# First batch of a retention and gMLP kernel: spatial columns 1 and 3 as seven products over pairs of blocks

## The chip, the cores and the metric

The kernel runs on one core of a Trainium2 chip. The time is the device time of one execution in microseconds; three executions were timed. Five engines work side by side, each through its own queue in order: TensorE (PE in the profile; PEld is its loading of weights), VectorE (DVE), ScalarE (ACT), GpSimd (POOL) and SyncE (SP), which here only issues DMAs.

## The reference

Two layers, for 4 batches of 768 positions. The first is a retention layer with 8 heads of 64:

```python
state = gamma * state + k[t] v[t]^T
y[t]  = scale * q[t] state            # x = y, heads side by side: 768 x 512
```

The second is a gated MLP whose gate mixes positions:

```python
h = relu(x @ w_in);  u, v = halves of h           # 512 columns each
v_n = (v - mean) / sqrt(var + 1e-6)               # over the columns
v_s = w_spatial @ v_n + b_spatial                 # over the 768 positions
out = (u * v_s) @ w_out
```

## The kernel before, in words

**Precision.** Most large products are done three times on split numbers: an operand is cut into a high part (rounded to fp32r by a copy on ACT) and a low part (the rest, a subtraction called `residue`), and high x high, high x low and low x high are added in PSUM (`split3`, L445). A product on whole float32 operands needs no split but more time on PE for each instruction.

**Retention.** Positions come in groups of 128, six to a batch (g = 0 to 23). `ret_set(g)` (S in the order text, L342) makes the scores of group g+1 and the state updates of group g, the two interleaved on PE; the updates read the values of group g, which must have been scaled by the decay. It ends with the scaling of the values of group g+1 on POOL (`scale_values`, L289) and the mask on DVE. `ret_out(g)` (X, L438) makes the output of the group: small 64x64 matmuls on PE, eviction into xf on DVE, xh on ACT (`out_half`, L429) and xl on POOL. The xh and xl of three groups (384 positions, one half of a batch) share one tile; there are two buffers of each, so the third half takes the buffer of the first when everything that reads that one is done.

**MLP.** `mlp_u(b, j, half)` (u or U, L579) makes block j (128 columns) of u, transposed, for one half of the positions: 12 matmuls and a relu on ACT. `units` numbers the pairs: 0 to 3 are the blocks in half 0, 4 to 7 in half 1. `v_products` (V) makes v for one group of positions; relu, mean and variance, a power on POOL and the normalisation (N) follow. `mlp_out` (o, O, L641) adds the part of one unit to the output of its half, in three PSUM banks, and stores the half after its fourth unit.

**The spatial product.** v_s of a block of columns is a product over six blocks of positions, in two halves of the output. There are two ways in the code. `spatial_products` (P, L598) takes one unit: six whole float32 matmuls, or 18 split ones where the column block has been split before by `norm_split` (D, L502). `combine` and `product` (C, L514, and M, L540) take a pair of column blocks p and p+2 in both halves: Winograd's form of Strassen's scheme, seven products of half size instead of eight, each of nine split matmuls. Its left sides are pieces of v_n, some of them sums made in place on POOL, copied on ACT and subtracted on DVE; its right sides are the spatial weight's quarters and their sums and differences, made once by `split_spatial` (W0 to W6, L224): for each of three rows a copy on ACT and a residue on DVE, ahead of them a sum on DVE for W3 to W6. W3 to W6 overwrite the whole weight or read overwritten parts, so a `spatial_products` on whole numbers must come before them. Batches 1 to 3 use the seven products for both pairs (columns 0 and 2, then 1 and 3).

**Batch 0 before.** Its four units of half 0 go by whole numbers in START (P1, P0, P3, P2). In FIRST, `item` (I4 to I7, L674) does unit 4 whole and units 5 to 7 on columns split by D1 to D3. W0 to W6 are spread over all of FIRST.

**Order.** The order is written out by hand in the texts START, FIRST, REST and LAST: each word is an action, carried out in turn when the program is built. In START every instruction is tied to the one before it on its engine. From FIRST on, only matmuls, loads, the splits of the weights and the scaling of values are tied (`tc.keep_in_program_order`): a tied instruction is queued behind whatever the text put before it on that engine, tied or not. The rest is placed by a scheduler at build time. S, X, G and J of FIRST with number n mean group n; batch 0 is being finished there while groups 7 to 13 of batches 1 and 2 are loaded and the retention of batch 1 runs (S6 to S12, X6 to X11, V0 to V5).

**Weights.** The input and output weights come as 64-bit floats, in twelve parts ("doubles", L139): loaded to a raw tile (L), made into two float32 parts by operations on ACT and DVE (a, c), rounded to the high part on ACT (H), and the rest computed by two subtractions and additions (R n, on POOL, or R 20+n, on DVE). Parts 4 to 7 are the column blocks of u's weight, 8 to 11 the row blocks of the output's.

**Buffers.** PSUM: two banks for scores and states, three for u, v, spatial products and, from FIRST on, the retention outputs, three for the outputs. The tag u has six buffers, t three, v three (v before its normalisation and output tiles share it), ca four (pieces, and W6's differences). Values of groups 2, 5 and 8 lie in the tile "third", in the room that W4's parts take later.

Of the kernel before, what the change touches and what calls it, by code (L numbers as in the profile page):

```python
# [10 lines left out]
F32R = mybir.dt.float32r  # L11
# [12 lines left out]
START = (  # L24
# [10 lines left out]
)  # L35
FIRST = (
    "S6 W0 I4 W1 D1 X6 J9 S7 G9 D2 I5 X7 J10 G10 D3 W2 S8 W3 I6 X8 S9 V0 G11 W4 I7 X9 J11 S10 "
    "G12 O7 N0 X10 W5 V1 V2 V3 N1 N2 J12 G13 S11 X11 J13 G14 V4 N3 S12 N4 V5 W6 N5"
)
# [22 lines left out]
def tile_retention_gmlp(  # L62
# [15 lines left out]
    P = 128  # L78
# [41 lines left out]
    def keep(ins):  # L120

        if fixed:
            tc.keep_in_program_order(ins)
# [9 lines left out]
    def residue(eng, out, whole, high):  # L133
        return eng.tensor_tensor(out, whole, high.bitcast(F32), ALU.subtract)  # L134

    def pick(n):
# [4 lines left out]
        for w, src in ((winv_w, w_inv), (winu_w, w_inu), (wout_w, w_out))  # L141
        for k in range(KT)
    ]
# [22 lines left out]
    def pair_room(dtype, name):  # L166
        return mpool.tile([P, 2, HC, P], dtype, tag="ca", name=name, bufs=4)

    rooms = []
    for n in ROOMS:  # L170
        t = slot(n, F32, f"room{n}").rearrange("p s c -> p (s c)")
        rooms += [t[:, :DM], t[:, DM : 2 * DM]]
    halves = {}

    def split_top(i):
# [48 lines left out]
    def split_spatial(n):  # L224
# [20 lines left out]
        for s in range(HC):  # L245
            tc.keep_in_program_order(nc.scalar.copy(high[:, s], wholes[s]))
            tc.keep_in_program_order(residue(nc.vector, low[:, s], wholes[s], high[:, s]))

# [252 lines left out]

    def norm_split(j):  # L502

        whole = vn[0][:, :, j * P : j * P + P]
        high, low = (
            pair_room(F32R, f"vn{i}_{j}").rearrange("p n s d -> p (n s) d") for i in range(2)
        )
        keep(nc.scalar.copy(high, whole))
        keep(residue(nc.vector, low, whole, high))
        columns[j] = high, low  # L510

    pieces = {}
# [60 lines left out]

    columns = {}
    gate = {}
# [22 lines left out]
    def spatial_products(b, j, half):  # L598
        dcol = slice(j * P, j * P + P)
        pp = ps_m.tile([P, DM], F32, tag="m", name=f"sp{b}_{j}_{half}")  # L600
        if not (half and j in columns):
            for s in range(NC):
                l, r = vn[b][:, s, dcol], whole_sp[half, s // HC][:, s % HC]
                mm(pp[:, :HALF], l, r, start=(s == 0), stop=(s == NC - 1))
        else:
            vh, vl = columns[j]
            split3(
                [
                    (
                        (vh[:, s], vl[:, s]),  # L610
                        tuple(parts_sp[s // HC][i][:, s % HC] for i in range(2)),
                    )
                    for s in range(NC)
                ],
                pp[:, :HALF],
            )
        gate[b, half, j] = pp

    def gate_product(b, j, half):
        pp, u = gate[b, half, j], us.pop((b, half, j))  # L620
        t = mpool.tile([P, HALF], F32, tag="t", name=f"t{b}_{j}_{half}", bufs=3)
        cols = slice(half * HALF, half * HALF + HALF)
        keep(nc.vector.tensor_tensor(t, pp[:, :HALF], bsp_t[:, cols], ALU.add))
        keep(nc.vector.tensor_tensor(t, t, u, ALU.mult))
        gate[b, half, j] = t

# [44 lines left out]
    units = [(j, half) for half in range(2) for j in range(NJ)]  # L671
    NU = len(units)

    def item(b, i):  # L674
        mlp_u(b, *units[i])
        if i + 1 < NU:
            mlp_u(b, *units[i + 1])
        spatial_products(b, *units[i])
        gate_product(b, *units[i])
        part_gate(b, i)  # L680
        if i > 0:
            mlp_out(b, *units[i - 1])

    actions = {
# [7 lines left out]
        "N": lambda b, g, n: mlp_norm(b + 1, n),  # L692
        "I": lambda b, g, n: item(b, n),
        "O": lambda b, g, n: mlp_out(b, *units[n]),
        "D": lambda b, g, n: norm_split(n),
        "m": lambda b, g, n: load(mask_t, mask),
# [127 lines left out]
```

## Time and profile before

| | us |
|---|---|
| median of three runs | 374.7 (374.28 to 374.99) |
| the profiled execution | 374.61 |
| its span | 372.8 |
| mean granted clock of TensorE | 0.994 of full |

| stage on PE | start, us |
|---|---|
| first u block of batch 0 (u0) | 49.99 |
| first whole spatial block (P1) | 54.18 |
| end of u3; o2 follows | 78.00 |
| whole block of unit 4 | 85.52 |
| last v group of batch 1 (V5), end | 144.56 |
| first of the seven products of batch 1 | 159.19 |

The span runs from the first to the last instruction of the program; what lies around it in the profiled execution is 374.61 - 372.8 = 1.8 us. In the profile a line number is often that of a helper: L126 is every matmul, L134 every residue. A name such as `u<-xh,winu_w` says which tile is written and which are read, and a mean over a group can mix several uses. Names of PSUM tiles tell the stage: s and d are scores and state changes, x retention outputs, sp the products of `spatial_products`, y, z and w the banks of the seven products. A whole float32 matmul shows as two records, so 24 of them are x48.

### The profile page before, as it was taken

The page shows a single profiled execution, that of the slowest core. Times are in us where ns is not written, and L with a number is a line of the kernel's source. Part 1 is how long each engine was busy: PE and PEld are TensorE (multiplying, and loading weights), DVE is VectorE, ACT ScalarE, POOL GpSimd, SP SyncE. Part 2 cuts the span into 40 slices and gives each one's busy share as a digit, 9 for nine tenths or more (in the row PEclk, how much of TensorE's full clock was granted, in tenths as well). Part 3 has the DMA queues.
Part 4 walks back from the last instruction along what each step waited for, and adds up shares of the span by engine and source line. Part 5 has one row for each costly group of instructions (what it writes and reads, how often), then busy time and mean ns, then how long its engine had stood idle before and what let it go on. Part 6 is the DMA issues. An engine that isn't in the chain of part 4 may idle for free.

```text
span 372.8 us, 10291 instructions
## 1 busy us (share of the span) xinstructions
PE 362.0 (97%) x4418; PEld 317.3 (85%) x4418; DVE 236.4 (63%) x513; ACT 154.5 (41%) x308; POOL 134.4 (36%) x131
## 2 busy tenths in 40 slices
PE   6899999999999999999999999999999999999996
PEld 2778785787998878999998888999997888999985
DVE  3989989995887876677674543367674433165530
ACT  2486682264433535533124444432323445432232
POOL 1354650001343523526424451327424341325042
PEclk9899999999999999999999999999999999999999
DMA  7997783001431721113305332021504002000022
GB/s 265 411 371 278 243 310 156 0 2 54 147 114 58 273 89 69 54 61 109 122 2 199 114 114 86 8 106 47 185 0 143 2 2 86 0 0 2 0 86 85
DMA packets 13581, 41.49 MB, mean 111 GB/s; under 512 B 1888, under 2 KB 2144, under 8 KB 13536
## 3 DMA queue, kind: packets, MB, share of 16 engines
q1 hardware_dynamic: 13392, 40.71, 30.0%
q8 instruction: 35, 0.57, 0.6%
q10 hardware_dynamic: 144, 0.13, 0.1%
q14 instruction: 10, 0.08, 0.1%
HBM read 34.54 MB, written 6.29 MB: 110 GB/s over the span
## 4 chain that ended last, share of the span: by engine, by line
PE 94%; DMA 3%; issue 1%; DVE 1%; POOL 0%; SPq 0%; ACT 0%; POOLq 0%
PE u L126 18%; PE v L126 18%; PE o L126 18%; PE y L126 10%; PE sp L126 8%; PE x L126 7%; PE z L126 5%; PE s L126 3%; PE d L126 3%; PE w L126 3%; DMA qk<-in_groups_dram 2%; DMA vd_t<-in_vdecay_dram 2%; PE total L126 1%; PE o_last L126 0%; POOL vk L298 0%
## 5 line engine op out<-in xcount | busy, mean ns | idle before, releaser
L126 PE MATMUL u<-xh,winu_w 128*128 128x384 f32 x256 | 68.1, 338 | 0.0
L126 PE MATMUL v<-winv_w,xh 128*128 128x512 f32 x192 | 60.6, 397 | 0.2 <-issue 0.2
L126 PE MATMUL o<-wout_w,gh 128*128 128x512 f32 (+1 forms) x192 | 60.5, 396 | 0.0
L126 PEld LDWEIGHTS u<-xh,winu_w 128*128 128x128 f32 x256 | 46.5, 188 | 0.8
L126 PE MATMUL u<-xl,winu_w 128*128 128x384 f32 x128 | 42.9, 335 | 0.0
L134 POOL TENSOR_TENSOR xl<-xf,xh 128x512 fp32r<-128x512 f32 x21 | 29.0, 1380 | 37.6 <-ACT xh L436 37.6
L126 PEld LDWEIGHTS v<-winv_w,xh 128*128 128x128 f32 x192 | 35.2, 188 | 8.1 <-issue 0.4
L126 PE MATMUL y<-sp,a 128*128 128x384 f32 x216 | 41.6, 336 | 0.0
L126 PEld LDWEIGHTS o<-wout_w,gh 128*128 128x128 f32 x192 | 35.2, 188 | 7.3
L534 ACT CAST a<-vn 128x384 fp32r<-128x384 f32 x42 | 21.6, 513 | 46.0 <-PE y L126 16.9
L134 POOL TENSOR_TENSOR gl<-ur,gh 128x384 fp32r<-128x384 f32 x24 | 26.8, 1116 | 37.7 <-ACT gh L630 37.2
L134 DVE TENSOR_TENSOR a<-vn,a 128x384 fp32r<-128x384 f32 x42 | 24.4, 580 | 24.6 <-ACT a L534 24.2
L126 PEld LDWEIGHTS y<-sp,a 128*128 128x128 f32 x216 | 38.1, 188 | 0.2
L126 PE MATMUL v<-winv_w,xl 128*128 128x512 f32 x96 | 37.5, 390 | 0.0
L126 PE MATMUL o<-wout_w,gl 128*128 128x512 f32 (+1 forms) x96 | 37.3, 389 | 0.0
L477 DVE BATCH_NORM_STATS2 bst<-vr 128x6 f32<-128x512 f32 x24 | 16.6, 691 | 29.3 <-ACT vr L470 29.1
L419 DVE SCALAR_TENSOR_TENSOR xf<-x,qg_t,qd_t 128x128 f32<-128x128 f32 x96 | 27.1, 343 | 10.3 <-PE x L126 10.3
L484 POOL TENSOR_TENSOR rs<-rs,mhalf 128x1 f32<-128x1 f32 x24 | 13.7, 573 | 44.0 <-DVE rs L479 41.8
L126 PE MATMUL s<-qk 64*64 64x64 f32 x768 | 27.4, 221 | 0.7 <-DMA qk<-in_groups_dram 0.7
L126 PEld LDWEIGHTS s<-qk 64*64 64x64 f32 x768 | 25.1, 137 | 2.9 <-DMA qk<-in_groups_dram 1.4
L500 ACT ACTIVATE vn<-vr,nb,rs 128x512 f32<-128x512 f32 x24 | 19.4, 814 | 17.4 <-DVE nb L489 16.4
L595 ACT ACTIVATE ur<-u 128x384 f32<-128x384 f32 x32 | 15.7, 490 | 25.9 <-PE u L126 25.7
(103 smaller groups left out, 669.8 us busy)
## 6 DMA issues: line engine op xcount, KB each, us to landing
qk<-in_groups_dram SPq DMA_DIRECT2D x24, 512.0 KB, 5.3
vk<-in_groups_dram SPq DMA_DIRECT2D x21, 512.0 KB, 4.4
out_dram<-ot SPq DMA_DIRECT2D x23, 256.0 KB, 2.1
wst<-in_w_sp_dram SPq DMA_DIRECT2D x4, 576.0 KB, 8.1
raw<-in_w_inv_dram SPq DMA_DIRECT2D x4, 512.0 KB, 6.5
raw<-in_w_inu_dram SPq DMA_DIRECT2D x4, 512.0 KB, 7.5
raw<-in_w_out_dram SPq DMA_DIRECT2D x4, 512.0 KB, 5.1
third<-in_groups_dram SPq DMA_DIRECT2D x3, 512.0 KB, 6.0
```

Of the source, the lines that this page charges most:

```text
L126: ins = nc.tensor.matmul(out, lhs, rhs, start=start, stop=stop, skip_group_check=shared)
L134: return eng.tensor_tensor(out, whole, high.bitcast(F32), ALU.subtract)
L419: nc.vector.scalar_tensor_tensor(xf[:, hp], t[hp % 2][:, hp // 2].rearrange("p i c -> p (i c)"), qg_t[:, c, hp : hp + 1], qd_t[:, hp], ALU ...
L477: keep(nc.vector.bn_stats(st, norm[b, c][0]))
L484: keep(nc.gpsimd.tensor_tensor(rs, rs, mhalf, ALU.pow))
L500: keep(nc.scalar.activation(vn[b][:, c], v, AF.Identity, bias=nb, scale=rs))
L534: nc.scalar.copy(t[:, 0], whole)
L595: keep(nc.scalar.activation(u, pu[:, :HALF], AF.Relu))
```

## The change

In batch 0, column blocks 0 and 2 keep the whole float32 way, in both halves, all in START (P2, P0, P6, P4). Column blocks 1 and 3 are done by the seven products of `combine` and `product` with b = 0 and p = 1, in FIRST, after W0 to W5 (W6 lies among the products). Of the three residues of each W, those of rows 0 and 2 go to POOL (`POOLED`); row 1 stays on DVE. u blocks 0 and 2 of both halves are computed in START (u0, u2, u4, u6), blocks 1 and 3 in FIRST (U5, U1, U7, U3). To suit this, the parts of u's and the output's weights are taken in the order 0, 2, 1, 3. `norm_split` and `item` go away; `gate_product` writes into u's buffer instead of t's. The low part of the output weights' last part moves from DVE to POOL (R31 to R11), two of the four low parts of the gate in START move to FIRST on POOL, and some words in the early part of START change places.

```diff
--- before.py
+++ after.py
@@ -22,20 +22,21 @@
 
 
 START = (
-    "L0 G0 a0 c00 c01 H0 v c02 m q0 L2 j0 p0 t00 k00 y00 y01 t01 R20 G1 L1 p1 a2 G2 c20 E0 q1 "
-    "h0 k01 c21 j1 t10 y10 a1 H2 k10 G3 c10 y11 p22 t11 c22 q2 c11 k11 c12 L3 l0 H1 q3 t20 k20 "
-    "E1 G4 R1 V00 j2 h1 t21 l11 p23 k21 y20 y21 L5 R2 j3 q4 t30 E2 a3 h2 j4 c30 V10 p24 V01 V11 "
-    "V02 L4 l12 c31 V20 a5 k30 y30 c32 t31 H3 k31 c50 G5 y31 q5 E3 t40 a4 j5 R3 V21 V12 k40 c40 "
-    "L6 c51 y40 p25 y41 t41 h3 l3 V03 a6 k41 c41 E4 c42 c52 r0 s0 G6 h4 l4 H4 V22 L8 R4 V13 V23 "
-    "r2 K0 t50 k50 y50 q6 s2 w2 r1 y51 E5 w0 p26 h5 s1 L9 V30 l15 V40 n0 N0 K1 L7 H5 V31 K2 B "
-    "n2 c60 a8 V32 V50 V33 V51 w1 V41 V42 c61 r3 n1 s3 H6 R5 N1 V52 L10 V43 N2 w3 n3 r4 s4 V53 "
-    "w4 r5 N3 s5 w5 n4 n5 c62 c80 R26 N4 N5 a7 c70 u0 a9 G7 c90 u1 j6 c91 a10 P1 c100 g1 P0 c81 "
-    "c82 H8 R28 P3 f1 g0 K3 L11 c101 f0 H10 d10 c92 H9 P2 c102 o0 R29 R30 c71 d11 H7 u2 c72 R27 "
-    "a11 g2 f2 d12 c110 c111 o1 G8 u3 g3 H11 c112 f3 d13 o2 R31"
+    "L0 G0 a0 c00 c01 H0 v c02 m q0 L2 j0 p0 t00 k00 y00 y01 t01 R20 G1 L1 p1 a2 G2 c20 E0 q1 h0 "
+    "k01 j1 t10 c21 y10 H2 a1 k10 G3 c10 y11 p22 t11 c11 c22 q2 k11 c12 L3 l0 H1 q3 t20 k20 E1 G4 "
+    "R1 V00 j2 h1 t21 l11 p23 k21 y20 y21 L5 R2 j3 q4 t30 E2 a3 h2 j4 c30 V10 p24 V01 V11 V02 L4 "
+    "l12 c31 V20 a5 k30 y30 c32 t31 H3 k31 c50 G5 y31 q5 E3 t40 a4 j5 R3 V21 V12 k40 c40 L6 c51 y40 "
+    "p25 a6 y41 t41 h3 l3 V03 k41 c41 E4 c42 c52 r0 s0 G6 h4 l4 H4 V22 L8 R4 V13 V23 r2 K0 t50 k50 "
+    "y50 q6 s2 w2 r1 y51 E5 w0 p26 h5 s1 L9 V30 l15 V40 n0 N0 K1 L7 H5 V31 K2 B n2 c60 a8 V32 V50 "
+    "V33 V51 w1 V41 V42 r3 n1 c61 s3 H6 R5 N1 V52 L10 V43 N2 c80 w3 n3 r4 s4 V53 w4 r5 N3 s5 w5 n4 "
+    "n5 c62 R26 N4 N5 a7 c70 u0 a9 G7 K3 c90 u2 j6 a10 P2 c100 c91 g2 P0 c81 H8 P6 f2 c92 g0 c82 "
+    "L11 c101 f0 H10 R28 d10 H9 P4 c102 o0 R29 c71 R30 d12 H7 u4 c72 R27 a11 g4 c110 c111 o2 c112 "
+    "G8 u6 g6 H11 R11"
 )
 FIRST = (
-    "S6 W0 I4 W1 D1 X6 J9 S7 G9 D2 I5 X7 J10 G10 D3 W2 S8 W3 I6 X8 S9 V0 G11 W4 I7 X9 J11 S10 "
-    "G12 O7 N0 X10 W5 V1 V2 V3 N1 N2 J12 G13 S11 X11 J13 G14 V4 N3 S12 N4 V5 W6 N5"
+    "U5 S6 U1 W0 X6 U7 W1 S7 G9 U3 W2 J9 X7 G10 J10 S8 W3 V0 X8 C11 W4 G11 V1 S9 W5 C15 C16 V2 M11 "
+    "C13 W6 M15 C17 M16 C12 M13 C14 M17 M12 M14 F1 N0 O1 F3 N1 X9 J11 S10 G12 O3 N2 F4 F6 V3 O4 O6 "
+    "X10 J12 F5 G13 N3 S11 O5 X11 J13 F7 V4 O7 V5 S12 G14 N4 N5"
 )
 REST = (
     "U0 U2 C01 U4 C05 C06 U1 U3 C03 X0 J2 S1 U6 G3 M01 C07 M05 C02 M06 C04 M03 M07 M02 C11 M04 "
@@ -139,7 +140,7 @@
     doubles = [
         (w[:, k, 0], w[:, k, 1], src[:, k])
         for w, src in ((winv_w, w_inv), (winu_w, w_inu), (wout_w, w_out))
-        for k in range(KT)
+        for k in (range(KT) if w is winv_w else (0, 2, 1, 3))
     ]
     raws = {}
 
@@ -171,6 +172,7 @@
         t = slot(n, F32, f"room{n}").rearrange("p s c -> p (s c)")
         rooms += [t[:, :DM], t[:, DM : 2 * DM]]
     halves = {}
+    POOLED = {(n, s) for n in range(7) for s in (0, 2)}
 
     def split_top(i):
         parts = raws.pop(i).bitcast(I32).rearrange("p (n w) -> p n w", w=2)
@@ -244,7 +246,7 @@
         parts_sp[n] = high, low
         for s in range(HC):
             tc.keep_in_program_order(nc.scalar.copy(high[:, s], wholes[s]))
-            tc.keep_in_program_order(residue(nc.vector, low[:, s], wholes[s], high[:, s]))
+            tc.keep_in_program_order(residue(nc.gpsimd if (n, s) in POOLED else nc.vector, low[:, s], wholes[s], high[:, s]))
 
     queries = {}
     keys = {}
@@ -499,16 +501,6 @@
         v, nb, rs = norm.pop((b, c))
         keep(nc.scalar.activation(vn[b][:, c], v, AF.Identity, bias=nb, scale=rs))
 
-    def norm_split(j):
-
-        whole = vn[0][:, :, j * P : j * P + P]
-        high, low = (
-            pair_room(F32R, f"vn{i}_{j}").rearrange("p n s d -> p (n s) d") for i in range(2)
-        )
-        keep(nc.scalar.copy(high, whole))
-        keep(residue(nc.vector, low, whole, high))
-        columns[j] = high, low
-
     pieces = {}
 
     def combine(b, p, m):
@@ -571,7 +563,6 @@
         gate_high(b, j, half)
         gate_low(b, j, half, nc.gpsimd)
 
-    columns = {}
     gate = {}
     us = {}
     acc = {}
@@ -598,22 +589,9 @@
     def spatial_products(b, j, half):
         dcol = slice(j * P, j * P + P)
         pp = ps_m.tile([P, DM], F32, tag="m", name=f"sp{b}_{j}_{half}")
-        if not (half and j in columns):
-            for s in range(NC):
-                l, r = vn[b][:, s, dcol], whole_sp[half, s // HC][:, s % HC]
-                mm(pp[:, :HALF], l, r, start=(s == 0), stop=(s == NC - 1))
-        else:
-            vh, vl = columns[j]
-            split3(
-                [
-                    (
-                        (vh[:, s], vl[:, s]),
-                        tuple(parts_sp[s // HC][i][:, s % HC] for i in range(2)),
-                    )
-                    for s in range(NC)
-                ],
-                pp[:, :HALF],
-            )
+        for s in range(NC):
+            l, r = vn[b][:, s, dcol], whole_sp[half, s // HC][:, s % HC]
+            mm(pp[:, :HALF], l, r, start=(s == 0), stop=(s == NC - 1))
         gate[b, half, j] = pp
 
     def gate_product(b, j, half):
@@ -621,8 +599,8 @@
         t = mpool.tile([P, HALF], F32, tag="t", name=f"t{b}_{j}_{half}", bufs=3)
         cols = slice(half * HALF, half * HALF + HALF)
         keep(nc.vector.tensor_tensor(t, pp[:, :HALF], bsp_t[:, cols], ALU.add))
-        keep(nc.vector.tensor_tensor(t, t, u, ALU.mult))
-        gate[b, half, j] = t
+        keep(nc.vector.tensor_tensor(u, t, u, ALU.mult))
+        gate[b, half, j] = u
 
     def gate_high(b, j, half):
         t = gate[b, half, j]
@@ -669,18 +647,6 @@
                 (nc.scalar if n else nc.sync).dma_start(out[b, rows, c], ot[:, c])
 
     units = [(j, half) for half in range(2) for j in range(NJ)]
-    NU = len(units)
-
-    def item(b, i):
-        mlp_u(b, *units[i])
-        if i + 1 < NU:
-            mlp_u(b, *units[i + 1])
-        spatial_products(b, *units[i])
-        gate_product(b, *units[i])
-        part_gate(b, i)
-        if i > 0:
-            mlp_out(b, *units[i - 1])
-
     actions = {
         "S": lambda b, g, n: ret_set(g + n),
         "Z": lambda b, g, n: ret_set(g + n, update=False),
@@ -690,9 +656,7 @@
         "W": lambda b, g, n: split_spatial(n),
         "K": lambda b, g, n: load_spatial(n),
         "N": lambda b, g, n: mlp_norm(b + 1, n),
-        "I": lambda b, g, n: item(b, n),
         "O": lambda b, g, n: mlp_out(b, *units[n]),
-        "D": lambda b, g, n: norm_split(n),
         "m": lambda b, g, n: load(mask_t, mask),
         "v": lambda b, g, n: [load(vd_t, vdecay), load(qg_t, qgroup), load(qd_t, qdecay)],
         "B": lambda b, g, n: load(bsp_t, b_sp),
```

## The prediction

> **What bounds the kernel now.** I read the page from the top, then the busy time by stretch, then the chain that ended last.
>
> ```profile
> span 372.8 us, 10291 instructions
> PE 362.0 (97%) x4418; PEld 317.3 (85%) x4418; DVE 236.4 (63%) x513; ACT 154.5 (41%) x308; POOL 134.4 (36%) x131
> PE 94%; DMA 3%; issue 1%; DVE 1%; POOL 0%; SPq 0%; ACT 0%; POOLq 0%
> 0.00:40.00 40.00, 33.24 (x749) 26.19 (x752) 31.60 (x62) 22.95 (x62) 14.71 (x16) 0.96 0.85 314
> 40.00:78.00 38.00, 38.00 (x231) 29.32 (x224) 34.31 (x76) 18.71 (x38) 10.84 (x12) 1.00 0.47 168
> 78.00:104.00 26.00, 26.00 (x403) 22.21 (x403) 20.39 (x42) 12.82 (x26) 4.67 (x4) 1.00 0.25 86
> 104.00:145.00 41.00, 40.67 (x643) 34.55 (x642) 30.93 (x74) 18.21 (x33) 18.65 (x17) 1.00 0.36 129
> ```
>
> The last four rows give, after the window's length, busy us of PE, PEld, DVE, ACT, POOL. TensorE (PE) is the bound. It idles 6.8 us in the first 40 us and almost never afterwards: 0.33 us from 40 to 145 us, the stretch that holds the whole first batch. So matmul time taken out of that stretch is worth its full length, unless a new wait of PE appears. The other engines have room on average; POOL worked only 4.67 of the 26 us from 78 to 104, exactly where the change sends it new work. Full shares don't show whether its order holds, so that is looked at apart.
>
> **The matmul time that goes.** Rows of the chain: start, length, what.
>
> ```profile
> 54.18 15.48 PE sp L126 x48
> 85.52 3.87 PE sp L126 x12
> 95.60 3.12 PE sp L126 x18
> 105.22 3.12 PE sp L126 x18
> 115.53 3.15 PE sp L126 x18
> ...
> 183.13 1.59 PE y L126 x9
> 192.56 1.59 PE y L126 x9
> 194.15 2.09 PE o L126 x9
> ```
>
> A block of columns in one half of the positions, in whole float32, costs 15.48 / 4 = 3.87 us; a block from split parts costs 3.12 us. Before, batch 0 has five of the first and three of the second: 15.48 + 3.87 + 3.12 + 3.12 + 3.15 = 28.74 us. After, P2, P0, P6, P4 stay whole (4 x 3.87 = 15.48), and the four block-halves of columns 1 and 3 become seven products of nine matmuls. Batch 1 does just that for its second pair: from 183.13 to 194.15, 11.02 us. Sum 26.50 us: **2.24 us less**.
>
> **What the new order does to PE's joints.**
>
> ```profile
> 69.66 2.08 PE o L126 x9
> 71.74 2.09 PE u L126 x12
> 78.00 2.08 PE o L126 x9
> 91.48 0.86 PE x L126 x48
> 93.29 2.31 PE u L126 x12
> 100.79 1.09 PE x L126 x64
> 102.94 2.28 PE u L126 x12
> 126.28 8.42 PE v L126 x36
> 134.69 0.02 issue
> 137.57 2.95 PE v L126 x12
> 144.56 10.43 PE u L126 x60
> ```
>
> A u group behind large matmuls takes 2.09 us, behind the 64x64 ones 2.28 to 2.31: a joint costs 0.2 us. FIRST's text had 8 such joints and has 10 (S6, S7, S8, X8, S9, S10, S11, X11, S12, X6, each ahead of a large group): **+0.4 us**. An X and S pair takes 102.94 - 100.79 = 2.15 us, but from 134.69 to 137.57, 2.88 us pass for S11 and X11: X11 stands right behind S11 and waits for its states. The new text puts O5 (2.08 us) between them, which covers it: **-0.73 us**. So far 2.24 - 0.4 + 0.73 = 2.57 us gained, about 372.0 us.
>
> **What is added in front of it.** Groups first (busy us, mean ns of one, idle ahead), then three groups with the shortest, median and longest ns, and two single instructions of POOL's timeline.
>
> ```profile
> L134 DVE TENSOR_TENSOR sp<-wst,sp 128x384 fp32r<-128x384 f32 x18 | 10.6, 635 | 2.6 <-ACT sp L246 2.5
> L532 POOL TENSOR_TENSOR vn<-vn 128x384 f32<-128x384 f32 x18 | 19.5, 1084 | 15.2 <-DVE a L134 12.6 <-ACT vn L500 2.5
> L484 POOL TENSOR_TENSOR rs<-rs,mhalf 128x1 f32<-128x1 f32 x24 | 13.7, 573 | 44.0 <-DVE rs L479 41.8 <-ACT vn L500 1.7 <-DVE nb L489 0.5
> L419 DVE SCALAR_TENSOR_TENSOR xf<-x,qg_t,qd_t 128x128 f32<-128x128 f32 x96 | 27.1, 343 | 10.3 <-PE x L126 10.3
> L134 POOL TENSOR_TENSOR df<-df,winu_w 128x512 f32<-128x512 f32 x2 | 2.6, 1288 | 1.0 <-ACT winu_w L207 1.0
> L624 DVE TENSOR_TENSOR t<-t,ur 128x384 f32<-128x384 f32 x8 | 4.5, 557 | 0.4
> L134 POOL TENSOR_TENSOR gl<-ur,gh x24: 999/1015/1342, 167.9 to 365.4; 128x384 fp32r<-128x384 f32 x24
> L134 POOL TENSOR_TENSOR xl<-xf,xh x21: 1275/1293/2289, 14.6 to 304.4; 128x512 fp32r<-128x512 f32 x21
> L436 ACT CAST xh<-xf x24: 608/621/624, 13.2 to 303.7; 128x512 fp32r<-128x512 f32 x24
> 95.41 1.29 POOL L134 TENSOR_TENSOR xl<-xf,xh 128x512 fp32r<-128x512 f32 x1 [3.12 <-ACT xh L436]
> 96.66 1.04 POOL L298 TENSOR_TENSOR third<-third,vd_t 128x512 f32<-128x512 f32 x1
> ```
>
> Fourteen spatial residues go from DVE (635 ns) to POOL. POOL never did this one; a gl residue has its shape, so 1.02 us (999 to 1342 ns). DVE is relieved of 8.9 us, worth nothing by itself, since PE is the bound. All splits now stand ahead of the products.
>
> Now the queue. A residue of W, and the scaling of the next group's values, are tied behind whatever the text put before them on POOL. The last two rows show it: scaling of group 8 (the tile third) starts the moment xl of group 6 is done. The new text reads X6, W1, S7, so POOL's order is xl of group 6, **two residues of W1**, scaling of group 8. And xl needs xh of group 6, which takes the buffer of batch 0's first half; u blocks 1 and 3 of that half still read it. Before, all four such u ran in START; now U1 and **U3** are in FIRST, and U3 stands behind X6, U7 and S7. Who waits at the end: S8, whose updates read group 8's scaled values, and with S8 all of PE, because its order is fixed.
>
> Times, with the rows above. The end of START holds the same groups as before (four u, four whole blocks, two o), so FIRST begins at 78.00. U5 2.09, S6 (2.15 - 1.09) 1.06, U1 2.28, X6 0.86, U7 2.28, S7 0.95 (93.29 - 91.48 - 0.86), U3 2.28: U3 ends at 89.80. X7 (1.09) ends at 90.89; there S8 wants to start. But after 89.80: handover 0.05 (assumed), xh 0.62, handover 0.05, xl 1.29, residues 2 x 1.02, scaling 1.04: 94.89. **PE waits 4.0 us.** With the shortest rows it is 3.9; with xl at 2289 ns and residues at 1342 ns 5.6. A cover that I can't exclude (xh free sooner) makes it 0. I take 4.0, since each link has a near row.
>
> Once S8 is through, the later parts are pressed but not clearly late. W5's residues come after W2, W3 and W4 on POOL; 94.9 + 8 residues (8.2) + xl 7 and 8 (2.6) + scaling of 9 and 10 (2.1) + two powers (2 x 0.57 = 1.1) ends near 109. M16, which reads W5, would start at 94.9 + S8 1.06, V0 to V2 with joints (3 x 2.95), X8 1.09, S9 1.06, M11 and M15 (3.1) = 110.1. That just fits, if the sums of C15 and C16 (L532's 1084 ns each, three of them) run while POOL waits for U3.
>
> **Edits taken at nothing.** Order 0, 2, 1, 3 of the weights: the same loads in the same places, each read no sooner than before. R11 on POOL instead of DVE: two operations at about 1.29 us (L134 df), begun at START's end by my estimate, so done near 81 us, ahead of the queue's wait. Gate product into u's buffer, dropped column splits (D), POOL gates of units 4 and 6: all under PE's 38 full microseconds and late use. K3 stands between G7 and L11 on SP in both texts, so its queue keeps its order. If DVE's cover (34.31 of 38 us) broke, u6 would lose up to a gate product, 2 x 0.56 = 1.1 us. The small swaps early in START lie where PE idles anyway; I take 0, between half a microsecond gained and lost.
>
> **Sum.** -2.24 + 0.4 - 0.73 + 4.0 = +1.4 us. The profiled execution took 374.61 us (span 372.8 and 1.8 around it), the median of the runs is 374.7; the forecast is **376.2 us**.
>
> **Rivals.**
>
> *The hold doesn't bind (faster).* One place decides: POOL's xl of group 6. If it starts before 90.89 - 1.04 - 2.04 - 1.29 = 86.5, scaling is done when PE comes to S8, and 372.1 us remains. X6 ends at 84.3 and DVE's four evictions (4 x 0.34) at 85.7, so without the hold by U3 this is what happens. For it: PE runs such products without a wait in batches 1 to 3, and had 0.33 us idle here. Against it: U3 after X6 is in the text, and in the later batches U3 stands ahead of X0. 371.5 to 373.3.
>
> *POOL is late a second time (slower still).*
>
> ```profile
> 104.54 1.34 DVE L233 TENSOR_TENSOR wst<-wst,wst 128x1152 f32<-128x1152 f32 x1
> 104.75 2.29 POOL L134 TENSOR_TENSOR xl<-xf,xh 128x512 fp32r<-128x512 f32 x1 [2.18 <-ACT xh L436]
> ```
>
> POOL's xl took 2.29 instead of 1.29 us while DVE formed a spatial sum: it lost about what was left of DVE's 1.34. If C15 and C16 don't go ahead, 3 x 1.08 = 3.3 us come behind W5, M16 waits about that long, and the clashes add to it: 376.2 + 3.3 = 379.5 us (377.8 to 381.5). [...]
>
> *A shorter wait that cancels the gain.* Should START end earlier, or one residue of W1 hide in xl's wait, S8 waits 2 to 3 us: 374.1 to 375.4.
>
> **How the numbers follow.** Forecast 0.45 (375.4 to 377.8), no hold 0.26, late twice 0.18, cancelled 0.11. A change under 0.2% (0.75 us) is about what a measurement can't tell from none. Forecast and late twice are slower, save 0.03 of the forecast's low end, which joins the cancelled ones: slower 0.60, same 0.14, faster 0.26. The range goes from 371.8, into the case without hold, to 380.0, which leaves out about 0.06 below and 0.09 above.
>
> **What would show it.** Right: sp at about 15.5 us with 63 more matmuls of y, z, w; then POOL in the order xl, two sp residues, third, with xl starting only after u block 3 ends near 90; and some 4 us of PE idle before group 8's updates, put down to POOL's scaling. Wrong: xl near 86; scaling of group 8 ahead of W1's residues; PE idle instead before z or the second y (late pieces), or none between 78 and 115 us. A START that ends off 78.0 would make the moved lines matter that I set to nothing.

## The result and the profile after

| | before, us | after, us |
|---|---|---|
| median of four runs each | 374.85 (374.28 to 375.42) | 379.61 (379.29 to 380.23) |
| the profiled execution, its span | 374.61, 372.8 | 379.29, 377.5 |

The change makes the kernel slower: the ratio is 1.0127, with a 95% interval of 1.0115 to 1.014. That is 4.8 us, where 1.5 us were forecast.

The page of the changed kernel, its engines and the shares of its chain:

```profile
PE 363.5 (96%) x4415; PEld 317.7 (84%) x4415; DVE 233.6 (62%) x502; ACT 154.9 (41%) x312; POOL 160.4 (42%) x153
...
PE 88%; DVE 6%; DMA 2%; POOL 1%; ACT 1%; issue 1%; SPq 1%; DVEq 0%; ACTq 0%
```

TensorE's share of the chain fell from 94% to 88%, and DVE's rose from 1% to 6%. The busy time by stretch says where (the columns as before: busy us of PE, PEld, DVE, ACT, POOL, then the granted clock, the DMA share and GB/s):

```profile
40.00:78.00 38.00, 38.00 (x186) 28.96 (x181) 35.37 (x78) 18.53 (x38) 11.05 (x13) 1.00 0.44 166
78.00:104.00 26.00, 23.30 (x502) 19.20 (x500) 22.73 (x42) 13.48 (x30) 24.07 (x20) 1.00 0.32 103
104.00:126.00 22.00, 20.99 (x215) 18.45 (x216) 19.93 (x40) 9.42 (x19) 14.83 (x15) 0.92 0.05 13
126.00:150.00 24.00, 24.00 (x328) 19.71 (x327) 9.01 (x28) 10.06 (x18) 10.69 (x12) 1.00 0.51 186
```

PE is full up to 78 us and from 126 us on. Between them, where the retention of batch 1 runs and the seven products are prepared and done, it lacks 2.70 + 1.01 us, and part of what is left runs at a lower clock (0.92 on average; the last section has more on it). There DVE is busy for 42.7 of 48 us and POOL for 38.9. All of PE's waits from 40 us to the end:

```profile
PE v L127 <- POOL xl L135: 1.1, 1, 1.1
PE v L127 <- ACT xh L438: 1.0, 1, 1.0
PE d L127 <- POOL third L300: 0.6, 1, 0.6
PE x L127 <- DVE ws L376: 0.5, 1, 0.5
PE d L127 <- issue: 0.4, 1, 0.4
PE y L127 <- DVE a L135: 0.2, 1, 0.2
```

The forecast was one wait of 4 us. Instead there is a row of short ones, the longest at V2. Rows of the chain that ended last (start, length, what):

```profile
49.17 4.18 PE u L127 x24
53.35 15.48 PE sp L127 x48
...
75.08 4.17 PE u L127 x24
...
80.35 2.29 PE u L127 x12
...
83.85 2.33 PE u L127 x12
...
87.27 2.30 PE u L127 x12
89.58 0.68 DVE third L342
...
116.14 1.49 PE y L127 x7
...
120.79 2.09 PE o L127 x9
...
148.36 10.63 PE u L127 x60
```

From 89.58 to 116.14 us this chain holds no matmul. Of these 26.6 us, 18.7 are work of DVE, 4.3 of POOL and 1.8 of ScalarE, and the rest are gaps between one and the next. In this stretch TensorE no longer sets the pace.

**The books.** u0 starts at 49.17 (49.99 before), and START's end, u6, is at 75.08 + 2.08 = 77.16, which is the forecast 28.0 us later. From there to batch 1's five u blocks are 71.2 us; before it was 144.56 - 78.00 = 66.6, and without any wait the prediction's terms give 66.6 - 2.57 = 64.0. So FIRST lost 7.2 us. The difference of the spans, 4.7 us, is -0.8 (u0 earlier) - 2.57 + 7.2 + 0.9 (spread over the later 229 us, 0.2 of it in the row of 60).

Along PE's order the 7.2 us arise like this: 0.6 up to the end of u block 3 at 89.57, with no wait at all; 1.9 from there to the end of S8 (the waits of 0.5 and 0.6 and the order around them); 1.3 more before V2; 2.7 inside V2; about 1 in the seven products. That makes 7.5; from O1 on PE takes a few tenths less than the terms give. As the parts are read off the pipelined matmuls, they hold to a few tenths.

To compare kernels without what stands ahead of u0, whose start differs from execution to execution, the stretch from u0 to batch 1's five u blocks is used below: 94.57 us before, 92.0 worked out for the change without waits, 148.36 - 49.17 = **99.2** after.

### The profile page after: what moved, and what is told of

The parts are those of the page before. It is cut to its first block, busy times and chain, and to the rows that moved or that the text cites. A ratio compares the mean times of both kernels' runs of the same rounds, so it can differ in the third digit from the quotient of the medians.

```text
span 377.5 us, 10311 instructions
## 1 busy us (share of the span) xinstructions
PE 363.5 (96%) x4415; PEld 317.7 (84%) x4415; DVE 233.6 (62%) x502; ACT 154.9 (41%) x312; POOL 160.4 (42%) x153
## 4 chain that ended last, share of the span: by engine, by line
PE 88%; DVE 6%; DMA 2%; POOL 1%; ACT 1%; issue 1%; SPq 1%; DVEq 0%; ACTq 0%
PE u L127 18%; PE o L127 18%; PE v L127 16%; PE y L127 11%; PE x L127 6%; PE z L127 5%; PE sp L127 4%; PE s L127 4%; PE w L127 3%; PE d L127 2%; DMA raw<-in_w_inv_dram 2%; PE total L127 1%; DVE sp L135 1%; SPq L132 1%; DVE xf L421 1%
## 5 line engine op out<-in xcount | busy, mean ns | idle before, releaser
L127 PE MATMUL v<-winv_w,xh 128*128 128x512 f32 x192 | 61.6, 402 | 1.1 <-ACT xh L438 1.0
L135 DVE TENSOR_TENSOR a<-vn,a 128x384 fp32r<-128x384 f32 x49 | 31.9, 651 | 29.2 <-ACT a L526 28.6
L135 POOL TENSOR_TENSOR gl<-ur,gh 128x384 fp32r<-128x384 f32 x30 | 32.5, 1083 | 41.0 <-ACT gh L608 40.6
L127 PE MATMUL y<-sp,a 128*128 128x384 f32 x252 | 49.1, 338 | 0.2 <-DVE a L135 0.2
L526 ACT CAST a<-vn 128x384 fp32r<-128x384 f32 x49 | 25.1, 513 | 52.0 <-POOL vn L524 23.9
L127 PEld LDWEIGHTS y<-sp,a 128*128 128x128 f32 x252 | 44.7, 189 | 1.0 <-DVE a L135 0.5
L127 PE MATMUL v<-winv_w,xl 128*128 128x512 f32 x96 | 38.4, 400 | 1.1 <-POOL xl L135 1.1
L608 ACT CAST gh<-ur 128x384 fp32r<-128x384 f32 x32 | 16.4, 512 | 38.3 <-DVE ur L558 18.1
L524 POOL TENSOR_TENSOR vn<-vn 128x384 f32<-128x384 f32 x21 | 23.0, 1098 | 15.7 <-DVE a L135 12.9
L127 PE MATMUL s<-qk 64*64 64x64 f32 x768 | 28.3, 225 | 1.2 <-DMA qk<-in_groups_dram 1.2
```

The costliest lines, as they stand in the source:

```text
L127: ins = nc.tensor.matmul(out, lhs, rhs, start=start, stop=stop, skip_group_check=shared)
L524: nc.gpsimd.tensor_tensor(*sums[m])
L526: nc.scalar.copy(t[:, 0], whole)
L608: keep(nc.scalar.copy(gh, t))
```

## The experiments

The theory after the result, called **deadline** here: all seven splits, the sums, the pieces and the retention of groups 6 to 9 have to pass DVE and POOL before the products, and the two together can't do it in time, whoever does what. Its rivals are the prediction's own step (the **order** of POOL behind U3's hold), START's swaps, and residues on POOL as such. A diff is against the changed kernel unless it says "before". Each median stands beside that of the kernel before on the same chip.

### The residues all on DVE, and all on POOL

```diff
-    POOLED = {(n, s) for n in range(7) for s in (0, 2)}
+    POOLED = set()
```

> The changed kernel with all 21 spatial residues back on DVE, POOL's 14 gone. Theory POOL (the wait ahead of the products comes from the residues in POOL's queue and from their clash with DVE): the 7.2 us that PE loses between 77 and 121 us shrink to 3 or less, so 375.5 us or below. Theory deadline (the vector work ahead of the products is too much for the TensorE work that stands there, whichever engine does it; DVE was busy 22.7 of 26 us already): 379 us or more, with the waits now put down to DVE.

Measured: 385.13 us against 374.85, ratio 1.0278 (1.0257 to 1.0298); the stretch takes 104.2 us. PE's longest wait is now 2.7 us, for a state update on DVE.

```diff
-    POOLED = {(n, s) for n in range(7) for s in (0, 2)}
+    POOLED = {(n, s) for n in range(7) for s in range(3)}
```

> The changed kernel with all 21 residues on POOL. Theory of one shared door (a POOL residue blocks DVE's operations on two SBUF tiles for its whole length, so 1.02 us on POOL is no better than 0.55 us on DVE once both are full): slower than 379.6, 380.5 to 383 us. Theory of two free engines (DVE is the late one, POOL has room): faster, 376 to 379 us.

Measured: 382.51 us against 375.12, ratio 1.021 (1.0172 to 1.0248); the stretch 102.0 us. The busy time by stretch, all on DVE first, then all on POOL:

```profile
78.00:104.00 26.00, 22.52 (x436) 19.27 (x435) 23.16 (x40) 13.09 (x29) 14.60 (x11) 0.93 0.29 88
104.00:126.00 22.00, 18.81 (x146) 16.03 (x144) 20.67 (x48) 8.67 (x18) 4.71 (x6) 0.92 0.05 18
```

```profile
78.00:104.00 26.00, 23.12 (x453) 19.54 (x455) 18.23 (x36) 13.46 (x31) 25.51 (x22) 0.93 0.31 103
104.00:126.00 22.00, 18.44 (x152) 15.43 (x148) 18.58 (x33) 8.77 (x18) 17.04 (x17) 1.00 0.00 1
```

With 0, 14 and 21 of the 21 residues on POOL the kernel takes 385.1, 379.6 and 382.5 us. In the first DVE is the one that has no room (43.8 of 48 us), in the last POOL (42.5 of 48, and 25.51 of the first 26). The changed kernel's share is the best of the three, and still late. Moving the residues to POOL was no mistake in itself: it gained 5.5 us on leaving them with DVE.

### POOL's residues where no product is near

The kernel before, with the same fourteen residues on POOL (diff against before):

```diff
-            tc.keep_in_program_order(residue(nc.vector, low[:, s], wholes[s], high[:, s]))
+            tc.keep_in_program_order(residue(nc.gpsimd if (n, s) in POOLED else nc.vector, low[:, s], wholes[s], high[:, s]))
```

> The kernel before with nothing changed but the engine of the residues: rows 0 and 2 of each W on POOL. There W2 to W6 are needed only by batch 1. Theory clash alone (POOL and DVE block each other wherever they meet, and PE feels it): 376 us or more. Theory deadline (clashes cost only where the products stand right behind the splits): within 0.5 us of the kernel before, 374.4 to 375.4 us.

Measured: 375.21 us against 374.85, ratio 1.0009 (0.9998 to 1.0019); the stretch 95.0 us. No difference can be measured: where no product stands right behind the splits, residues on POOL cost nothing that shows.

### The order of the prediction: scaling ahead of W1, and U3 ahead of X6

```diff
-    "U5 S6 U1 W0 X6 U7 W1 S7 G9 U3 W2 J9 X7 G10 J10 S8 W3 ...
+    "U5 S6 U1 W0 X6 U7 S7 W1 G9 U3 W2 J9 X7 G10 J10 S8 W3 ...
```

> The changed kernel with W1 and S7 exchanged in the text, so that the scaling of group 8 on POOL stands ahead of W1's two residues. Theory of the prediction (the tie of the scaling behind W1 is what PE waits for): the 0.64 us wait for the tile third goes and the groups behind it move up, 377.5 to 379.0 us. Theory deadline: POOL does the same work before the products, so what is won at S8 is lost again at V2: 379.3 to 380.0 us.

Measured: 379.29 us against 374.85, ratio 1.0118 (1.0097 to 1.014); the stretch 99.3 us. PE's wait before group 8's updates falls from 0.6 to 0.3 us and the 0.5 us at X7 go, but 0.8 us come up at X8, and V2's two waits stay (0.8 and 1.1). So the two residues between xl and the scaling are not the price.

```diff
-    "U5 S6 U1 W0 X6 U7 W1 S7 G9 U3 W2 J9 X7 G10 J10 S8 W3 ...
+    "U1 S6 U3 W0 X6 U5 W1 S7 G9 U7 W2 J9 X7 G10 J10 S8 W3 ...
```

> The changed kernel with U1, U3, U5, U7 in place of U5, U1, U7, U3, so that batch 0's first half is read for the last time 3.2 us earlier. If the prediction's hold is real (xh of group 6 waits until U3 has read its buffer): S8's wait goes, 376 to 378 us. If X6 simply takes whichever buffer is free first, as the trace suggests (xh started at 86.97 us, after U7 and during U3): no gain, 379.2 to 380.5 us.

Measured: 379.15 us against 374.93, ratio 1.011 (1.0085 to 1.0134); the stretch 99.2 us, as without the edit. The first copy of xh in ACT's timeline, in the changed kernel and then in this one:

```profile
86.97 0.62 ACT L438 CAST xh<-xf 128x512 fp32r<-128x512 f32 x1 [0.99 <-DVE xf L421]
```

```profile
86.73 0.62 ACT L438 CAST xh<-xf 128x512 fp32r<-128x512 f32 x1 [0.94 <-DVE xf L421]
```

In the changed kernel xh of group 6 is written from 86.97 on, while u block 3 reads batch 0's half 0 until 89.57: it can't be that buffer. In the other order it is written while U7 still reads half 1. So in both runs batch 1's first half takes the buffer that was freed first, and not always that of batch 0's first half, as the description of the kernel before has it; and in both the copy waited for DVE's eviction of x alone. The prediction's hold doesn't exist.

### Splits made ahead, in START

W0 and W1 are made in START, two residues of the output weights go to POOL to give DVE room for them, and the scaling comes ahead of W2:

```diff
-    "... H9 P4 c102 o0 R29 c71 R30 d12 H7 u4 c72 R27 a11 g4 c110 c111 o2 c112 G8 u6 g6 H11 R11"
+    "... H9 P4 R9 c102 o0 c71 R10 d12 H7 u4 c72 R27 a11 W0 g4 c110 c111 o2 c112 G8 W1 u6 g6 H11 R11"
-    "U5 S6 U1 W0 X6 U7 W1 S7 G9 U3 W2 J9 ...
+    "U5 S6 U1 X6 U7 S7 W2 G9 U3 J9 ...
```

> The changed kernel with W0 and W1 moved into START's end, the low parts of two output weights (R29, R30) given to POOL where it idles (54 to 76 us), and W2 behind S7. So 4.1 us of POOL and 1.1 us of DVE leave the stretch ahead of the products, 2.8 us of DVE leave START. Theory deadline (vector work ahead of the products): PE's loss of 7.2 us falls by 2.5 to 4.5 us, 375.0 to 377.2 us. Theory of a single chain (X8, eviction, xh, xl, V2 is late by itself): less than 1 us, 378.6 to 379.6 us.

Measured: 384.34 us against 374.85, ratio 1.025 (1.0212 to 1.0289). That is a miss: it was to gain and loses 4.7 us more. DVE's timeline, and then POOL's, in the same microseconds of START:

```profile
63.57 0.43 DVE L201 TENSOR_SCALAR room<-df 128x512 int32<-128x512 int32 x1
...
65.24 1.62 DVE L135 TENSOR_TENSOR gl<-ur,gh 128x384 fp32r<-128x384 f32 x1
66.78 1.75 DVE L206 SCALAR_TENSOR_TENSOR room<-raw,room 128x512 f32<-128x512 uint32 x1
...
70.27 1.40 DVE L201 TENSOR_SCALAR room<-df 128x512 int32<-128x512 int32 x1
71.59 0.55 DVE L135 TENSOR_TENSOR gl<-ur,gh 128x384 fp32r<-128x384 f32 x1
72.06 0.68 DVE L206 SCALAR_TENSOR_TENSOR room<-raw,room 128x512 f32<-128x512 uint32 x1
```

```profile
64.78 1.66 POOL L135 TENSOR_TENSOR df<-df,wout_w 128x512 f32<-128x512 f32 x1 [12.47 <-ACT wout_w L209]
...
69.76 1.62 POOL L216 TENSOR_TENSOR wout_w<-df,room 128x512 fp32r<-128x512 f32 x1
```

A residue of one shape takes DVE 1.62 us beside POOL's operations and 0.55 us once these are over, the operation after it 1.75 against 0.68. Four operations of DVE (one is left out here) lost about 4.2 us to the four that POOL had taken over, which DVE does in 0.7 us each: more lost than saved. This is the clash that the second rival spoke of, in a stretch where the forecast had seen none. PE's longest wait in this run, 3.2 us, is for the scaled values of a group, late on POOL; how the loss divides between the two was not taken apart.

### START's swaps, and the one gain in the order of FIRST, by themselves

The kernel before with only the swaps in the early part of START (diff against before, cut):

```diff
-    "... c20 E0 q1 h0 k01 c21 j1 t10 y10 a1 H2 k10 ... N2 w3 n3 r4 s4 V53 w4 r5 N3 s5 w5 n4 n5 c62 c80 R26 ...
+    "... c20 E0 q1 h0 k01 j1 t10 c21 y10 H2 a1 k10 ... N2 c80 w3 n3 r4 s4 V53 w4 r5 N3 s5 w5 n4 n5 c62 R26 ...
```

> The kernel before with only the early part of START (up to u0) in the changed kernel's order. The prediction set these swaps to nothing. In the changed kernel u0 starts at 49.17 instead of 49.99 us. If the swaps make that: 373.9 to 374.3 us and u0 near 49.2; if it comes from elsewhere: 374.85 us, u0 near 50.

Measured: 374.76 us against 375.12, ratio 0.9987 (0.9966 to 1.0009): no difference that can be measured. In the profiled executions of the changed kernel and of eight others with its START, u0 starts between 48.99 and 52.10 us, so the 0.8 us by which it came earlier in the changed kernel's own says nothing.

On top of it, V3 between S11 and X11, which should save the 0.7 us that the change saves there with O5:

```diff
-    "G12 O7 N0 X10 W5 V1 V2 V3 N1 N2 J12 G13 S11 X11 J13 G14 V4 N3 S12 N4 V5 W6 N5"
+    "G12 O7 N0 X10 W5 V1 V2 N1 N2 J12 G13 S11 V3 X11 J13 G14 V4 N3 S12 N4 V5 W6 N5"
```

> The kernel before with the early START order of the first run of this set and V3 moved between S11 and X11, which is the prediction's other gain without the seven products. If S11 and X11 really lose 0.73 us by standing together: 0.5 to 0.9 us below the first run of this set, 373.0 to 373.6 us. If the wait only moves on: no more than 0.2 us below it.

Measured: 374.71 us against 375.12, ratio 0.999 (0.9977 to 1.0004), no more than without V3's move. PE's wait at X11 is gone, but 0.5 us of waiting for the relu of v (ACT vr) comes up in its place.

### Spare matmuls in front of the waits

Nine 512-column matmuls ahead of S8 and nine ahead of V2, whose result nobody reads. If PE only waits there, they vanish in the waits.

```diff
-    "... J9 X7 G10 J10 S8 W3 V0 X8 C11 W4 G11 V1 S9 W5 C15 C16 V2 M11 "
+    "... J9 X7 G10 J10 T9 S8 W3 V0 X8 C11 W4 G11 V1 S9 W5 C15 C16 T9 V2 M11 "
...
+    def spare(n):
+        ps = ps_m.tile([P, DM], F32, tag="m", name="spare")
+        for i in range(n):
+            mm(ps, winv_h[:, i % KT, :P], winv_h[:, i % KT], start=i == 0, stop=i == n - 1)
```

> The changed kernel with 18 spare matmuls of 512 columns (some 0.23 us each, 4.2 us in all, their result is not used): nine ahead of S8, nine ahead of V2. Theory deadline (VectorE and GpSimd set the pace of this stretch, TensorE waits for them): the spare work is done while PE would wait and keeps its clock up, so it costs 0 to 1 us: 379.0 to 380.6 us. Theory TensorE (the loss is in PE's own work: joints, slow clock, order): the 4.2 us come on top: 383 to 384.5 us.

Measured: 382.21 us against 375.12, ratio 1.0189 (1.0159 to 1.0218); the stretch 101.4 us, so 2.2 us came on top of some 4.1 us that they need (a v group of twelve takes 2.74 us, and these are 18), and half was absorbed. PE's largest wait:

```profile
PE y L127 <- DVE t L548: 1.6, 1, 1.6
```

The result lies between the theories. The waits at S8 and V2 are gone, and new ones, of 1.6 and 0.7 us, stand at the products. The spare work ahead of S8 also delays S8, and the W sums that DVE may only start behind S8's and S9's masks; so a later start of PE makes the other engines later too. It does not show how much of the 7.2 us is pure waiting.

### Other hands: the low parts and the scaling by ScalarE

The low parts written by ScalarE, as copies (they hold the whole numbers, not the residues, so the output is another):

```diff
-            tc.keep_in_program_order(residue(nc.gpsimd if (n, s) in POOLED else nc.vector, low[:, s], wholes[s], high[:, s]))
+            tc.keep_in_program_order(nc.scalar.copy(low[:, s], wholes[s]))
```

> The changed kernel with the 21 spatial low parts written by a plain copy on ScalarE instead of a subtraction on VectorE or GpSimd (so the low parts hold the whole weight, and the output differs from the reference); everything else stays. 14.3 us of POOL and 3.9 us of DVE leave, ACT gains 10.7 us and has room (18.4 us busy from 78 to 104... of 48 us to 126). Theory deadline (the joint work of VectorE and GpSimd ahead of the products makes PE wait): PE's loss of 7.2 us falls below 1.5 us and the prediction's gain of 2.6 us comes out, 372.0 to 374.0 us. Theory order (ties, buffers or PE's own work): 377 us or more.

Measured: 377.68 us against 374.93, ratio 1.0062 (1.0045 to 1.008); the stretch 96.3 us, 2.9 of the 7.2 us back. What PE still waits for is partly ScalarE (1.0 us for the relu of v, 0.8 for a piece's copy), which now has 21 operations more. By the bounds set beforehand this run speaks for the order theory. But ScalarE was busy for 22.9 of the 48 us in the changed kernel already, not 18.4, and is for 31.6 here, so that it became late itself. The run decides neither way.

The scaling of groups 8 to 10 by ScalarE:

```diff
-            scale_values(g + 1)
+            scale_values(g + 1, nc.scalar if g + 1 in (8, 9, 10) else None)
```

> The changed kernel with the scaling of groups 8, 9 and 10 as eight small multiplications each on ScalarE (0.34 us each) instead of one of 1.04 us on POOL. POOL loses 3.1 us in the stretch and, with its clashes, DVE some of its blocked time. Theory deadline: 1 to 3 us less, 376.5 to 378.5 us. Theory order: 379.2 us or more; a loss would show that ScalarE's queue has become the late one.

Measured: 382.5 us against 374.93, ratio 1.02 (1.0173 to 1.0226), a miss. PE's longest wait, and a step of the chain ahead of it:

```profile
PE v L127 <- ACT vr L472: 3.5, 1, 3.5
```

```profile
93.21 5.12 DMA vk<-in_groups_dram
```

The scaling of group 9 stands in ScalarE's queue ahead of splits and the relu of v. Its values' DMA takes 5.1 us, ScalarE stands idle for 2.4 of them, and everything behind it waits along. In the changed kernel POOL comes to the same scaling at 97.06 us and doesn't idle for it. The run says nothing on the deadline.

### The residues left out

The last run takes away the 21 residues alone: no low part is computed, and the products read the high part in its place, with as many matmuls (the output is another).

```diff
-        high, low = (slot(SPLIT[n][i], F32R, f"sp{n}_{i}") for i in range(2))
-        parts_sp[n] = high, low
+        high = slot(SPLIT[n][0], F32R, f"sp{n}_0")
+        parts_sp[n] = high, high
...
-            tc.keep_in_program_order(residue(nc.gpsimd if (n, s) in POOLED else nc.vector, low[:, s], wholes[s], high[:, s]))
```

> The changed kernel without the 21 spatial residues at all: the products read the high parts in place of the low ones (same matmuls, other numbers, so the output differs from the reference), and no engine takes the work over. This frees 14.3 us of POOL and 3.9 us of DVE without loading ScalarE, which in the run with copies became late itself (PE waits of 1.0 and 0.8 us put down to ACT). The stretch from u0 to batch 1's five u blocks took 99.2 us in the changed kernel, 96.3 us with the copies, and would take 92.0 us with no wait at all. Theory deadline: 92.5 to 95.0 us for that stretch, and 373 to 376 us in all. Theory order (ties and short chains behind X8 and S9): 96 us or more, as with the copies, and 377 us or more in all.

Measured: 374.95 us against 374.93, ratio 0.9994 (0.9979 to 1.0009); span 373.7 us, the stretch 144.99 - 49.81 = 95.2 us. PE's waits from 40 us on:

```profile
PE y L127 <- DVE t L547: 0.7, 1, 0.7
PE x L127 <- issue: 0.5, 1, 0.5
PE v L127 <- POOL xl L135: 0.2, 1, 0.2
```

Without the residues the whole 4.7 us of the change are gone, and the granted clock is 1.00 from 40 to 150 us. The waits that were 1.1, 1.0 and 0.6 us are 0.2 us or nothing. The total lies in the deadline theory's range, the stretch 0.2 us above it and clear of the other's 96. So the loss hangs on the residues ahead of the products, as the deadline theory has it: on their work and on the time that DVE and POOL lose by blocking each other, which this run takes away together. Yet the result is 375.0 us and not the 372.1 worked out for a kernel without waits: of the 3.2 us by which the stretch is over 92.0, 1.5 us are idle time of PE, 0.6 us the joints (below), and about 1 us is assigned to nothing. Here too the chain holds no matmul from 92.03 to 117.63 us: evictions, masks, state updates and W sums fill DVE's queue even so.

No version tried is measurably faster than the kernel before.

## Why the prediction was right, and where not

**Right, in part by luck: sign and range.** Slower was the likeliest side, and 379.6 lies in the range, near its upper end. But the sign came from a wait of 4.0 us whose cause doesn't exist; without it the prediction's own terms give 372.1 us, faster. It was right by luck, and the range reaches so far because of the second rival. (The sum's terms give 374.7 + 1.43 = 376.1, not 376.2.)

**Right: the terms on PE.** The whole blocks take 15.48 us again. S11, O5, X11 and V4 run without a wait: from O1 to batch 1's u blocks are 148.36 - 120.79 = 27.6 us, within a few tenths of what the sum with the 0.73 us gives. The weights' new order and R11 left no wait of PE in 40 to 78 us.

**Mis-sized: the joints.** The steps S6, U1, X6, U7, S7 and U3, which hold the joints, took 0.6 us more than forecast. X6 was taken at 0.86 and takes 83.85 - (80.35 + 2.29) = 1.21 us, and S7 was taken at 0.95 and takes 87.27 - (83.85 + 2.33) = 1.09. Both figures had come from an X and an S that stood as a pair; here each stands alone between two u groups.

**Wrong: the hold.** The step that failed is that xh of group 6 "takes the buffer of batch 0's first half; u blocks 1 and 3 of that half still read it". It took the other buffer, and the wait before S8, forecast at 4.0 us, was 0.6 us. POOL's timeline of the changed kernel:

```profile
87.66 1.58 POOL L135 TENSOR_TENSOR xl<-xf,xh 128x512 fp32r<-128x512 f32 x1
89.20 2.28 POOL L135 TENSOR_TENSOR sp<-wst,sp 128x384 fp32r<-128x384 f32 x2
91.44 1.04 POOL L300 TENSOR_TENSOR third<-third,vd_t 128x512 f32<-128x512 f32 x1
...
94.69 2.41 POOL L135 TENSOR_TENSOR xl<-xf,xh 128x512 fp32r<-128x512 f32 x1
```

The order xl, two residues, scaling of group 8 is the one forecast. But START ended 0.8 us sooner here, so the forecast puts xl at 89.7 and the scaling's end at 94.1; they came at 87.66 and 92.48, and S8 waited 0.6 us for them, after 0.5 us at X7. (The two handovers, assumed at 0.05 us each, were 0.10 us from the eviction to xh and 0.07 from xh to xl.) By the first rival's point (xl before 86.5, here 85.7) xl was 2.0 us late; what made it late is no buffer but DVE:

```profile
84.59 1.25 DVE L135 TENSOR_TENSOR sp<-wst,sp 128x384 fp32r<-128x384 f32 x1
85.76 1.11 DVE L421 SCALAR_TENSOR_TENSOR xf<-x,qg_t,qd_t 128x128 f32<-128x128 f32 x4
...
94.45 1.50 DVE L235 TENSOR_TENSOR wst<-wst,wst 128x1152 f32<-128x1152 f32 x1
...
96.89 1.43 DVE L235 TENSOR_TENSOR wst<-wst,wst 128x1152 f32<-128x1152 f32 x1
...
99.26 1.36 DVE L135 TENSOR_TENSOR sp<-wst,sp 128x384 fp32r<-128x384 f32 x1
...
101.14 1.10 DVE L421 SCALAR_TENSOR_TENSOR xf<-x,qg_t,qd_t 128x128 f32<-128x128 f32 x4
```

X6 ended at 83.85, but DVE evicted it only from 85.76 on, behind state updates and a residue of W0 that took 1.25 us; xl, the scaling and S8 came later by that. (X7's wait is for state updates, which stand behind a residue of W1 on DVE; with W1 behind S7 it went.) X8 ended before V1 began at 97.87 and was evicted from 101.14 on, behind a W sum of 1.43 us, state updates, a residue that took 1.36 us and the statistics of v. V2 then waited 0.96 us for its xh and 1.07 us for its xl. The forecast priced DVE's relief at nothing, "since PE is the bound", and put the moved work on POOL's queue alone. DVE's queue was the other half of the same limit: it kept seven residues, all W sums and all evictions. What its relief is worth shows in the run with all residues on DVE, which is 5.5 us slower. No run moved the W sums or the evictions within DVE's queue, so how much of the 7.2 us is their order there, how much work and how much blocking stays open.

**Right in kind: the second rival.** It gave 379.5 us for POOL late a second time, with clashes between DVE and POOL. The mechanism is there, but not its place: M16 did not wait for W5's residues; V2 waited. That its figure is met so closely is luck. The groups by line of the changed kernel (busy us, mean ns of one):

```profile
L135 POOL TENSOR_TENSOR sp<-wst,sp 128x384 fp32r<-128x384 f32 x12 | 14.6, 1233 | 0.0
L135 DVE TENSOR_TENSOR sp<-wst,sp 128x384 fp32r<-128x384 f32 x6 | 6.0, 993 | 1.0 <-ACT sp L248 0.7
```

A residue on POOL was taken at 1.02 us and takes 1.23, and those left on DVE went from 635 to 993 ns. So twelve on POOL and six on DVE make 20.6 us of work, where 18 on DVE had made 10.6 before. One case stands in the timelines above: the xl at 94.69 took 2.41 us beside the W sum of 1.50 us at 94.45, 1.29 being its usual time.

## What to carry to other kernels

When work is moved ahead of a consumer, add up what each of the engines must finish by then, with the time that two of them lose by blocking each other (xl 2.41 us for 1.29 here), and compare it with the time to the deadline; the average share of an engine (POOL's 4.67 of 26 us here) doesn't tell it. An engine that doesn't set the bound still holds a queue, so look at what its evictions stand behind before a relief of it is called worth nothing. Where a forecast rests on a buffer being held, find in the trace which buffer such a tile takes.

## What the runs showed of the hardware

**The clock fell behind two short waits, in one run and not in another.** The busy time around V2, in the changed kernel and then with the order U1, U3, U5, U7:

```profile
102.00:105.50 3.50, 1.48 (x5) 0.96 (x6) 2.77 (x10) 1.11 (x2) 2.58 (x3) 1.00 0.00 0
105.50:109.00 3.50, 3.50 (x10) 2.75 (x10) 2.87 (x5) 1.53 (x4) 3.50 (x4) 0.51 0.02 5
```

```profile
102.00:105.50 3.50, 1.65 (x6) 1.07 (x7) 2.77 (x10) 1.11 (x2) 2.76 (x4) 1.00 0.00 0
105.50:109.00 3.50, 3.50 (x20) 3.19 (x19) 2.86 (x6) 1.84 (x4) 3.50 (x4) 1.00 0.02 5
```

In the changed kernel PE was busy for 1.48 of the 3.5 us from 102 us on, with no wait over 1.07 us, and then ran for 3.5 us at a granted 0.51, which lacks 0.49 x 3.5 = 1.7 us of full clock. V2 took 2.7 us too long by the second wait and the clock. From 109 to 112.5 us the clock was back at 1.00.

In the other run PE had the same two waits and was busy for 1.65 us, and the clock stayed at 1.00. The time wasn't shorter for that: PE then waited 1.4 us more at the products, for DVE:

```profile
PE y L127 <- DVE t L548: 1.4, 1, 1.4
```

The stretch takes 99.2 us in both runs. So no price of the fallen clock shows here: where it didn't fall, PE waited for DVE instead. What decides whether it falls isn't shown. With spare matmuls the longest wait was 1.6 us, and the clock stayed at 1.00.

**Beside POOL an operation of DVE with one input was slow too, and the evictions were not.** In the run with the splits in START, the TENSOR_SCALAR at 70.27, which reads one tile, took 1.40 us beside an addition on POOL; the same operation took 0.43 us at 63.57, with POOL idle. Of the operations that read two tiles, a spatial residue took 1.25 us at 84.59 in the changed kernel, beside POOL, and 0.55 us at 94.59 in the kernel before, with POOL idle. DVE's four evictions of x, which read PSUM, took 1.11 us at 85.76, beside two residues on POOL, and 1.10 us at 101.14, with POOL idle from 101.48 on.
